# Filter transform of a long convolution: second stage issued for two groups at a time, with more places for its buffers

## The chip, the cores and the metric

One Trainium2 chip, one of its cores. The metric is the device time of one execution in microseconds. The kernel before takes 899.78 us (median of three runs, 898.28 to 901.48).

## What is computed

```python
def _attn_ref(x, v, pos_emb, w1, w2):            # x, v: 4 x 12608 x 128
    h_mlp = np.maximum(pos_emb @ w1, 0.0) @ w2   # a filter of 12608 points for each of 128 channels
    h_filt = h_mlp * np.exp(-0.01 * pos)[:, None]
    u = x * v
    Uf = np.fft.rfft(u, n=2 * S, axis=1)
    Hf = np.fft.rfft(h_filt, n=2 * S, axis=0)
    y = np.fft.irfft(Uf * Hf[None], n=2 * S, axis=1)[:, :S]
    return x * y
```

The result then goes through a small expert layer: per batch the 128 rows with the highest score are put through two matrices (1024 wide) and added back. All of it is fp32.

## The kernel before, in words

The long transforms are split into two short ones by a two-factor index map (101 by 125 points), done as matmuls. Channels go in 32 **groups** of four. The program has four parts, one after the other: (1) the filter's values (`h_hid`, to about 33 us); (2) the **filter transform** (`h_spec`, about 33 to 110 us), which the change touches; (3) the main loop over 4 batches x 32 groups, which transforms, multiplies with the stored filter spectrum and transforms back; (4) the choice of rows and the expert layer, spread over the main loop, the last of it behind it.

`h_spec` does this for each group g:

- **fold** (L373, GpSimd; the first four on VectorE): adds and subtracts mirrored halves of the filter into one of four places `fb`.
- **First stage F(g)** (`fwd`, L382): 16 fp32 matmuls of 101 columns, recorded as 32 rows of the trace, into two PSUM banks: the pair a0, a1 for even g, c1 for odd g. ScalarE copies both banks to SBUF, `te` (L385, two copies). Then fold(g + 4) is issued.
- **Second stage S(g)** (L402): 64x64 tiles on four quarters of the array, here 8 fp32 matmuls of 202 columns (16 rows of the trace), from `te` into `p` and `q`, the two banks of c2 for even g and of c0 for odd g.
- ScalarE copies q to `qs` (L404). VectorE then does four operations, two of them with a mirrored operand: L407, L408 (in place on p), and twice L410, which read p and write the sums `ht`. SyncE stores `ht` to DRAM (`hd`, L411), from where the main loop loads it again.

TensorE runs its instructions in program order, so S(g) stands behind F(g + 1), and S(g) may write p only after VectorE has finished with S(g - 2) in the same banks. PSUM is full: a0, a1 (one bank each), c0, c1, c2 (two each). SBUF has two places for `te` and two for `ht`.

The main loop's first steps use the same banks: the first transform f(0) (L426) writes a0, a1, is copied by ScalarE (L428), and the second transform D(0) (L268) writes c1. VectorE then works on it (L435 to L447); D(1) goes to c0, D(2) to c1 again, f(1) and f(2) between them. From D(2) on TensorE also runs the inverse transforms (L263).

Of the kernel before, what the change touches and what calls it, by code (L numbers as in the profile page):

```python
# [17 lines left out]
B, S, D, FO = 4, 12608, 128, 64  # L18
NQ = 64
N1, N2, N3 = 101, 250, 125  # L20
# [3 lines left out]
NG = 32  # L24
HC = 4 * N1
# [14 lines left out]
JH = (N3 + 1) // 2  # L40
# [13 lines left out]
OFF, _o = {}, 0  # L54
# [33 lines left out]
def _steps():  # L88
    j = np.arange(N3)
    first = -(-(N1 * N3 - N1 * j) // N3)  # L90
    blk = [slice(32 * k, min(32 * k + 32, N3)) for k in range(NB)]
    return first, [(c, int(first[c].min()), int(first[c].max())) for c in blk]
# [71 lines left out]
def hyena_moe(ctx, tc, xg, x2, pos, bw, ww, wg, mw1, mw2, fo, c1, gx, cf, ci, wm, tk, out):  # L164
    nc = tc.nc
# [6 lines left out]
    arena = cp.tile([128, ARENA], F32, name="arena")  # L172
    big = cp.tile([128, D * 2 * NJ], F32, name="big")

    def view(t, off, shape):
        n = int(np.prod(shape[1:]))
        r = t[:shape[0], off:off + n]
        if len(shape) > 2:
            ax = "abcd"[:len(shape) - 1]
            r = r.rearrange(f"p ({' '.join(ax)}) -> p {' '.join(ax)}", **dict(zip(ax[1:], shape[2:])))  # L180
        return r

    def buf(name, k, shape):
        o, n, w = OFF[name]
        return view(arena, o + k % n * w, shape)
# [7 lines left out]
    def ps1(k, shape, name):  # L193
        return view((*bank1, *bank2[::2])[k], 0, shape)

    def ps2(k, shape, name):
        return view(bank2[k], 0, shape)
# [29 lines left out]
    hb = view(big, 0, [N1, 2, D, N3 + 1])  # L227
    fo_sb = view(arena, OFF["wx"][0] + 32 * JH, [128, 2, NQ])
    fbo = [OFF["wx"][0], OFF["wx"][0] + 16 * JH] + [OFF["xa"][0] + k * 8 * D for k in (2, 3)]
    hd = dp.tile([128, NG, 2 * HC], F32, name="hd")  # L230
    blk = [c for c, _, _ in _steps()[1]]

    def rev(t):
        return t.rearrange("p (s i) -> p s i", i=N1)[:, :, ::-1]

    def nat(t):
        return t.rearrange("p (s i) -> p s i", i=N1)

    def load_u(t):
        b, g = divmod(t, NG)  # L240
        if b < B:
            for k, n in enumerate("xv"):
                nc.sync.dma_start(buf(n, t, [NP, XC]), xg[b, :, g, k])

    def stage_u(t):
        if t >= B * NG:
            return
        x, v = buf("x", t, [NP, XC]), buf("v", t, [NP, XC])
        nc.gpsimd.tensor_tensor(out=x, in0=x, in1=v, op=ALU.mult)  # L249

    def load_h(t):
        if t < B * NG:
            nc.sync.dma_start(buf("ht", t, [128, 2 * HC]), hd[:, t % NG])

    def mm2(o, lhsT, rhs, **kw):
        kw = kw or dict(start=True, stop=True)
        w = 32 if spare[0] else NQ
        for a in range(0, 128, w):
            nc.tensor.matmul(o[a:a + w], lhsT=lhsT[:, a:a + w], rhs=rhs, **kw)
# [94 lines left out]
    def h_spec():  # L354
        te = {}

        def tps(g):
            if g % 2:
                t = ps2(1, [128, 2, 512], f"htp_{g}")
                return [t[:, e, :HC] for e in range(2)]  # L360
            return [ps1(e, [128, HC], f"htp_{g}_{e}") for e in range(2)]

        def pqs(g):
            t = ps2(0 if g % 2 else 2, [128, 2, 512], f"hpq_{g}")
            return [t[:, e, :HC] for e in range(2)]

        def fold(g, eng=nc.gpsimd):
            if g >= NG:
                return
            fb[g] = view(arena, fbo[g % 4], [N1, 2, 2, 4, JH])  # L370
            hg = hb[:, :, 4 * g:4 * g + 4]
            for k, op in enumerate((ALU.add, ALU.subtract)):
                eng.tensor_tensor(out=fb[g][:, k], in0=hg[:, :, :, :JH], in1=hg[:, :, :, N3:JH - 1:-1], op=op)  # L373

        def fwd(g):
            b = fb.pop(g)
            tp = tps(g)
            t = te[g] = buf("te", g, [128, 2, HC])
            for e in range(2):
                for s in range(4):  # L380
                    for w in range(2):
                        nc.tensor.matmul(tp[e][w * NQ:w * NQ + JH, s * N1:(s + 1) * N1], lhsT=b[:, w ^ e, e, s], rhs=c1_sb[:N1, 0],  # L382
                                         start=True, stop=True)
            for e in range(2):
                nc.scalar.copy(out=t[:, e], in_=tp[e])  # L385
            fold(g + 4)

        fb = {}
        for g in range(4):
            fold(g, nc.vector)  # L390
        fwd(0)
        for g in range(NG):
            if g + 1 < NG:
                fwd(g + 1)
            p, q = pqs(g)
            t = te.pop(g)
            for h in range(2):
                c = slice(h * 2 * N1, (h + 1) * 2 * N1)
                for e in range(2):
                    for w, o in enumerate((p, q)):  # L400
                        r = slice(w * NQ, w * NQ + JH)
                        nc.tensor.matmul(o[e * NQ:(e + 1) * NQ, c], lhsT=fo_sb[r, e], rhs=t[r, e, c], start=True, stop=True)  # L402
            qs = buf("qs", g, [128, HC])
            nc.scalar.copy(out=qs, in_=q)  # L404
            vs = buf("yz", g, [128, HC])
            ht = buf("sd", g, [128, 2, HC])
            nc.vector.tensor_tensor(out=nat(vs), in0=rev(p), in1=nat(qs), op=ALU.subtract)  # L407
            nc.vector.tensor_tensor(out=nat(p), in0=nat(p), in1=rev(qs), op=ALU.add)  # L408
            for e, op in enumerate((ALU.add, ALU.subtract)):
                nc.vector.tensor_tensor(out=ht[:, e], in0=p, in1=vs, op=op)  # L410
            nc.sync.dma_start(hd[:, g], ht.rearrange("p e c -> p (e c)"))  # L411
            if NG - 5 <= g < NG - 3:
                stage_u(g - NG + 5)
                load_u(g - NG + 7)
            if g == NG - 2:
                stage_u(2)
            if g >= NG - 3:
                load_h(g - NG + 3)
# [487 lines left out]
    class Experts:  # L906
# [36 lines left out]
        def second(self, yp, hs, c0, c1):  # L943
            for c in range(c0, c1):
                mm2(yp, hs[:, c], self.m2[:, c], start=(c == 0), stop=(c == 7))
# [85 lines left out]
    for t in bank2[2:] + bank1 + bank2[:2]:  # L1031
        nc.vector.memset(t, 0.0)
    h_hid()
    h_spec()
    ex = None
    te, uv, ys, sd, ph = {}, {}, {}, {}, {}
# [3 lines left out]
    for t in range(NT + LAG):  # L1040
        g = t % NG
# [3 lines left out]
        if t < NT:  # L1045
            pq = ps2(1 - t % 2, [128, 2, 512], f"pq_{t}")
# [18 lines left out]
            o = t - 1 in uv  # L1065
# [37 lines left out]
        if i >= 0 and i % NG in LA:  # L1103
            if i % NG == LA[0]:
                ph[b] = P1(b)
            k, e = divmod(LA.index(i % NG), 2)
# [42 lines left out]
def build(inputs):  # L1149
    import concourse.bacc as _bacc  # L1150
    nc = _bacc.Bacc("TRN2", target_bir_lowering=False, num_devices=1, dynamic_dma_scratch_size=4096)
    arrays, args = {}, []
    for name, a in _layout(inputs):
        arrays[f"in_{name}_dram"] = a
        args.append(nc.dram_tensor(f"in_{name}_dram", a.shape, mybir.dt.from_np(a.dtype), kind="ExternalInput").ap())
    args.append(nc.dram_tensor("out_0_dram", (B, PR, NJ, D), F32, kind="ExternalOutput").ap())
    with tile.TileContext(nc) as tc:
        hyena_moe(tc, *args)
    return nc, arrays
# [7 lines left out]
```

## Time and profile before

| | |
|---|---|
| median of three runs | 899.78 us |
| the profiled execution, its own time | 897.32 us |
| its span (first to last instruction) | 895.5 us |
| TensorE busy | 865.7 us, 97% of the span |
| VectorE busy | 807.6 us, 90% |
| filter transform, first to last L402 | 36.38 to 110.85 us |
| DMA over the span | 214 GB/s |

A row of the timeline gives the start, the length, the engine, the line of the kernel, the operation with out<-in and the shapes, how many instructions were merged (x...), and in brackets how long the engine stood idle before and what ended that. PE is TensorE, DVE is VectorE, ACT is ScalarE, POOL is GpSimd. A matmul's modelled end lies after the start of the next, so lengths of merged rows overlap; paces are read from starts.

### The profile page before, as it was taken

The page shows a single profiled execution, that of the slowest core. Times are in us where ns is not written, and L with a number is a line of the kernel's source. Part 1 is how long each engine was busy: PE and PEld are TensorE (multiplying, and loading weights), DVE is VectorE, ACT ScalarE, POOL GpSimd, SP SyncE. Part 2 cuts the span into 40 slices and gives each one's busy share as a digit, 9 for nine tenths or more (in the row PEclk, how much of TensorE's full clock was granted, in tenths as well). Part 3 has the DMA queues.
Part 4 walks back from the last instruction along what each step waited for, and adds up shares of the span by engine and source line. Part 5 has one row for each costly group of instructions (what it writes and reads, how often), then busy time and mean ns, then how long its engine had stood idle before and what let it go on. Part 6 is the DMA issues. An engine that isn't in the chain of part 4 may idle for free.

```text
span 895.5 us, 46412 instructions
## 1 busy us (share of the span) xinstructions
PE 865.7 (97%) x19606; PEld 763.4 (85%) x19606; DVE 807.6 (90%) x1543; ACT 627.9 (70%) x2242; POOL 763.9 (85%) x834
## 2 busy tenths in 40 slices
PE   8999989999999999999999999999999999999965
PEld 6788768999999889888899798888998898879954
DVE  8998899999999899999998898999998989997883
ACT  6655575555558988885579798855698888646920
POOL 5898659999999889898999798999998989988710
PEclk9999999999999999999999999999999999999996
DMA  7044587777887967688779766788797767855810
GB/s 251 35 174 172 205 291 226 213 217 230 262 248 246 296 219 220 200 247 250 243 234 299 224 213 207 231 247 236 250 300 237 221 199 227 253 176 179 267 60 7
DMA packets 83512, 195.06 MB, mean 218 GB/s; under 512 B 9639, under 2 KB 46608, under 8 KB 83304
## 3 DMA queue, kind: packets, MB, share of 16 engines
q1 hardware_dynamic: 83048, 191.57, 67.6%
q8 instruction: 154, 2.52, 1.1%
q0 software_dynamic: 256, 0.52, 0.2%
q14 instruction: 54, 0.44, 0.2%
HBM read 151.46 MB, written 40.60 MB: 214 GB/s over the span
## 4 chain that ended last, share of the span: by engine, by line
PE 71%; DVE 16%; ACT 5%; POOL 4%; issue 3%; DMA 2%; POOLq 0%; DVEq 0%; SPq 0%; ACTq 0%
PE c L263 19%; PE a L426 15%; PE c L268 15%; ACT arena L601 4%; PE c L546 3%; PE a L542 3%; PE a L546 3%; PE c L542 3%; PE c L402 2%; PE a L382 2%; DVE arena L440 2%; DVE c L441 2%; PE c L382 2%; DVE arena L446 1%; DVE ms L696 1%
## 5 line engine op out<-in xcount | busy, mean ns | idle before, releaser
L263 PE MATMUL c<-ci_sb,arena 128*26 128x126 f32 x8128 | 261.0, 271 | 2.1 <-POOL arena L453 1.6
L263 PEld LDWEIGHTS c<-ci_sb,arena 128*26 128x26 f32 x8128 | 244.7, 104 | 5.1 <-POOL arena L453 1.8
L268 PE MATMUL c<-arena,cf_sb 128*32 128x404 f32 x2048 | 214.0, 502 | 3.3 <-ACT arena L428 1.3
L426 PE MATMUL a<-c_sb,arena 128*32 128x202 f32 (+1 forms) x4096 | 216.1, 334 | 0.0
L426 PEld LDWEIGHTS a<-c_sb,arena 128*32 128x32 f32 (+1 forms) x4096 | 174.5, 108 | 26.7 <-issue 12.8
L249 POOL TENSOR_TENSOR arena<-arena 128x500 f32<-128x500 f32 x128 | 161.9, 1265 | 11.3 <-DMA arena<-in_xg_dram 11.3
L428 ACT COPY arena<-a 128x404 f32<-128x404 f32 x256 | 128.1, 501 | 50.2 <-PE a L426 48.8
L477 ACT COPY big<-c 128x824 f32<-128x824 f32 x127 | 106.3, 837 | 78.2 <-PE c L263 77.9
L453 POOL TENSOR_TENSOR arena<-arena 128x404 f32<-128x404 f32 x127 | 124.0, 977 | 39.0 <-DVE arena L447 30.7
L601 ACT ACTIVATE arena<-arena 128x128 f32<-128x128 f32 x502 | 147.4, 299 | 11.7 <-DVE arena L591 9.5
L268 PEld LDWEIGHTS c<-arena,cf_sb 128*32 128x32 f32 x2048 | 100.8, 109 | 35.6 <-issue 18.8
L440 DVE TENSOR_TENSOR arena<-c,arena 128x808 f32<-128x808 f32 x127 | 126.8, 998 | 3.8
L441 DVE TENSOR_TENSOR c<-c,arena 128x808 f32<-128x808 f32 x127 | 126.7, 998 | 0.0
L454 POOL TENSOR_TENSOR arena<-arena 128x404 f32<-128x404 f32 x127 | 123.6, 973 | 0.0
L601 ACT ACTIVATION_READ_ACCUMULATOR arena<-arena 128x1 f32 x502 | 96.0, 191 | 0.0
L529 POOL TENSOR_TENSOR arena<-big 128x512 f32<-128x512 f32 x72 | 89.8, 1285 | 0.7 <-PE c L542 0.4
L446 DVE TENSOR_TENSOR arena<-c,arena 128x404 f32<-128x404 f32 x127 | 73.6, 579 | 12.9
L435 DVE TENSOR_TENSOR c<-c,arena 128x404 f32<-128x404 f32 x128 | 74.6, 583 | 11.6 <-ACT arena L271 8.2
L432 DVE TENSOR_TENSOR c<-c,arena 128x404 f32<-128x404 f32 x128 | 75.0, 586 | 9.6 <-ACT c L765 4.9
L497 POOL TENSOR_TENSOR big<-big,arena 128x184 f32<-128x184 f32 x128 | 74.5, 582 | 10.0
L271 ACT COPY arena<-c 128x404 f32<-128x404 f32 x128 | 63.6, 497 | 24.2 <-PE c L268 23.1
L496 POOL TENSOR_TENSOR big<-big,arena 128x184 f32<-128x184 f32 x128 | 75.0, 586 | 1.3 <-ACT arena L478 1.3
(196 smaller groups left out, 1433.5 us busy)
## 6 DMA issues: line engine op xcount, KB each, us to landing
arena<-in_xg_dram SPq DMA_DIRECT2D x256, 250.0 KB, 3.9
arena<-hd SPq DMA_DIRECT2D x128, 404.0 KB, 4.5
out_dram<-arena SPq DMA_DIRECT2D x60, 420.0 KB, 5.4
arena<-in_x_dram SPq DMA_DIRECT2D x36, 420.0 KB, 4.7
hd<-arena SPq DMA_DIRECT2D x32, 404.0 KB, 3.0
arena<-in_x_dram SPq DMA_DIRECT2D x48, 210.0 KB, 5.0
arena<-in_pos_dram SPq DMA_DIRECT2D x15, 202.0 KB, 4.5
arena<-in_x_dram SPq DMA_DIRECT2D x4, 315.0 KB, 4.5
```

The costliest lines, as they stand in the source:

```text
L249: nc.gpsimd.tensor_tensor(out=x, in0=x, in1=v, op=ALU.mult)
L263: nc.tensor.matmul(o[32 * k:32 * k + c.stop - c.start], lhsT=lhsT[:, c], rhs=rhs, start=True, stop=True)
L268: nc.tensor.matmul(pq[w][a:a + 32], lhsT=cf_sb[:, 2 * w + a // NQ, a % NQ:a % NQ + 32], rhs=te[:, a // NQ], start=True, stop=True)
L426: nc.tensor.matmul(tps[s // 2][c, s % 2], lhsT=u[:, s, c], rhs=c1_sb[:, 0:k + 2:k + 1], start=True, stop=True)
L428: nc.scalar.copy(out=te[:, :, 2 * h:2 * h + 2].rearrange("p e s i -> p s e i"), in_=tps[h])
L440: nc.vector.tensor_tensor(out=mt, in0=uv, in1=ht[:, 0].unsqueeze(1).to_broadcast([128, 2, HC]), op=ALU.mult)
L441: nc.vector.tensor_tensor(out=uv, in0=uv, in1=ht[:, 1].unsqueeze(1).to_broadcast([128, 2, HC]), op=ALU.mult)
L453: eng.tensor_tensor(out=nat(sd[:, 0]), in0=nat(yz[:, 0]), in1=rev(yz[:, 1]), op=ALU.add)
L454: eng.tensor_tensor(out=nat(sd[:, 1]), in0=rev(yz[:, 0]), in1=nat(yz[:, 1]), op=ALU.subtract)
L477: nc.scalar.copy(out=ay[:, t % NG, :NJ + JM, ss], in_=o3[:, :, :NJ + JM].rearrange("p s x -> p x s"))
L529: nc.gpsimd.tensor_tensor(out=cm[:, e].rearrange("p j (g s) -> p j g s", s=4), in0=av[0], in1=av[1], op=op)
L601: nc.scalar.activation(out=x, in_=x, func=AF.Copy, accum_out=self.sc[:, j:j + 1])
```

## The change

The first stage runs two groups ahead in pairs: after the start, TensorE's order is F(2j+2), F(2j+3), S(2j), S(2j+1) instead of F(g+1), S(g). The second stage does all 404 columns in one matmul (4 instead of 8 matmuls for a group). `te` gets four places and `ht` gets four; the two new places of `te` and one of `ht` lie in a part of the arena that the main loop uses later, one of `ht` in the main loop's `mt`. The PSUM banks of both stages, the folds, ScalarE's and VectorE's operations and the stores stay as they are.

```diff
     fbo = [OFF["wx"][0], OFF["wx"][0] + 16 * JH] + [OFF["xa"][0] + k * 8 * D for k in (2, 3)]
+    teo = [OFF["te"][0], OFF["te"][0] + 2 * HC] + [OFF["xa"][0] + k * 8 * D for k in (0, 1)]
+    hto = [OFF["sd"][0], OFF["mt"][0], OFF["xa"][0] + 4 * 8 * D, OFF["sd"][0] + 2 * HC]
...
         def fwd(g):
             b = fb.pop(g)
             tp = tps(g)
-            t = te[g] = buf("te", g, [128, 2, HC])
+            t = te[g] = view(arena, teo[g % 4], [128, 2, HC])
...
-        fwd(0)
+        def second(g):
+            t = te.pop(g)
+            pq[g] = pqs(g)
+            for e in range(2):
+                for w, o in enumerate(pq[g]):
+                    r = slice(w * NQ, w * NQ + JH)
+                    nc.tensor.matmul(o[e * NQ:(e + 1) * NQ], lhsT=fo_sb[r, e], rhs=t[r, e], start=True, stop=True)
+
+        pq = {}
+        ahead = {0: (0, 1), 1: (2,), 2: (3, 4), 3: (5,)}
         for g in range(NG):
-            if g + 1 < NG:
-                fwd(g + 1)
-            p, q = pqs(g)
-            t = te.pop(g)
-            for h in range(2):
-                c = slice(h * 2 * N1, (h + 1) * 2 * N1)
-                for e in range(2):
-                    for w, o in enumerate((p, q)):
-                        r = slice(w * NQ, w * NQ + JH)
-                        nc.tensor.matmul(o[e * NQ:(e + 1) * NQ, c], lhsT=fo_sb[r, e], rhs=t[r, e, c], start=True, stop=True)
+            for k in ahead.get(g, (g + 2, g + 3) if g % 2 == 0 else ()):
+                if k < NG:
+                    fwd(k)
+            if g < 4:
+                second(g)
+            elif g % 2 == 0:
+                second(g)
+                second(g + 1)
+            p, q = pq.pop(g)
             qs = buf("qs", g, [128, HC])
             nc.scalar.copy(out=qs, in_=q)
             vs = buf("yz", g, [128, HC])
-            ht = buf("sd", g, [128, 2, HC])
+            ht = view(arena, hto[g % 4], [128, 2, HC])
```

TensorE in the middle of the filter transform, before: F(6), S(5), F(7), and the first matmul of S(6). a0 and a1 are one bank each, c0 to c2 two banks each, and the brackets name the engines whose semaphores the row waits for.

```order
L382 MATMUL a0_70<-c1_sb_80,arena_68 63x101 [waits Pool_49] x2
L382 MATMUL a0_70<-c1_sb_80,arena_68 63x101 x6
L382 MATMUL a1_71<-c1_sb_80,arena_68 63x101 x8
L402 MATMUL c0_72<-arena_68 64x202 [waits DVE_49,Activation_49]
L402 MATMUL c0_72<-arena_68 64x202
L402 MATMUL c0_72<-arena_68 64x202 [waits Activation_49]
L402 MATMUL c0_72<-arena_68 64x202 x5
L382 MATMUL c1_73<-c1_sb_80,arena_68 63x101 [waits Pool_49] x2
L382 MATMUL c1_73<-c1_sb_80,arena_68 63x101 x14
L402 MATMUL c2_74<-arena_68 64x202 [waits DVE_49,Activation_49]
```

The same place after the change: F(8), F(9), S(6), S(7).

```order
L384 MATMUL a0_70<-c1_sb_80,arena_68 63x101 [waits Activation_49,Pool_49]
L384 MATMUL a0_70<-c1_sb_80,arena_68 63x101 [waits Pool_49]
L384 MATMUL a0_70<-c1_sb_80,arena_68 63x101 x6
L384 MATMUL a1_71<-c1_sb_80,arena_68 63x101 [waits Activation_49]
L384 MATMUL a1_71<-c1_sb_80,arena_68 63x101 x7
L384 MATMUL c1_73<-c1_sb_80,arena_68 63x101 [waits Activation_49,Pool_49]
L384 MATMUL c1_73<-c1_sb_80,arena_68 63x101 [waits Pool_49]
L384 MATMUL c1_73<-c1_sb_80,arena_68 63x101 x14
L399 MATMUL c2_74<-arena_68 64x404 [waits DVE_49,Activation_49]
L399 MATMUL c2_74<-arena_68 64x404 x3
L399 MATMUL c0_72<-arena_68 64x404 [waits DVE_49,Activation_49]
L399 MATMUL c0_72<-arena_68 64x404 x3
```

The two second stages now stand side by side, each with a wait of its own for VectorE, and the two first stages stand ahead of both.

TensorE at the end of the filter transform, before: the last first stage F(31), then S(30) and S(31), then the main loop's f(0) (L426).

```order
L382 MATMUL c1_73<-c1_sb_80,arena_68 63x101 [waits Pool_49] x2
L382 MATMUL c1_73<-c1_sb_80,arena_68 63x101 x14
L402 MATMUL c2_74<-arena_68 64x202 [waits DVE_49,Activation_49]
L402 MATMUL c2_74<-arena_68 64x202
L402 MATMUL c2_74<-arena_68 64x202 [waits Activation_49]
L402 MATMUL c2_74<-arena_68 64x202 x5
L402 MATMUL c0_72<-arena_68 64x202 [waits DVE_49,Activation_49]
L402 MATMUL c0_72<-arena_68 64x202
L402 MATMUL c0_72<-arena_68 64x202 [waits Activation_49]
L402 MATMUL c0_72<-arena_68 64x202 x5
L426 MATMUL a0_70<-c1_sb_80,arena_68 32x202 [waits Pool_49]
```

The same place after the change: the last matmuls of F(31), then S(28), S(29), S(30), S(31), then f(0) (L436 there).

```order
L384 MATMUL c1_73<-c1_sb_80,arena_68 63x101 x14
L399 MATMUL c2_74<-arena_68 64x404 [waits DVE_49,Activation_49]
L399 MATMUL c2_74<-arena_68 64x404 x3
L399 MATMUL c0_72<-arena_68 64x404 [waits DVE_49,Activation_49]
L399 MATMUL c0_72<-arena_68 64x404 x3
L399 MATMUL c2_74<-arena_68 64x404 [waits DVE_49,Activation_49]
L399 MATMUL c2_74<-arena_68 64x404 x3
L399 MATMUL c0_72<-arena_68 64x404 [waits DVE_49,Activation_49]
L399 MATMUL c0_72<-arena_68 64x404 x3
L436 MATMUL a0_70<-c1_sb_80,arena_68 32x202 [waits Pool_49]
```

Four second stages with no first stage between them now stand ahead of the main loop's first matmuls; before there were two.

## Rows read from the trace of the kernel before

**Rows 1.** The profile's page, part 1: busy time, share of the span and instructions of each engine.

```profile
PE 865.7 (97%) x19606; PEld 763.4 (85%) x19606; DVE 807.6 (90%) x1543; ACT 627.9 (70%) x2242; POOL 763.9 (85%) x834
```

**Rows 2.** Timeline of TensorE, 59.9 to 64 us, one round of the filter transform.

```profile
61.06 1.61 PE L382 MATMUL a<-c_sb,arena 101*63 101x101 f32 x32
62.59 0.92 PE L402 MATMUL c<-arena 63*64 63x202 f32 x16
63.44 0.74 PE L382 MATMUL c<-c_sb,arena 101*63 101x101 f32 x12
```

**Rows 3.** Timeline of TensorE, 61.44 to 62.22 us, a piece from the middle of one first stage (12 pairs of matmuls, two side by side).

```profile
61.19 1.21 PE L382 MATMUL a<-c_sb,arena 101*63 101x101 f32 x24
```

**Rows 4.** Timeline of TensorE, 33 to 50 us, the start of the filter transform: a single matmul of the first stage, the first S(0), and S(4).

```profile
34.73 0.25 PE L382 MATMUL c<-c_sb,arena 101*63 101x101 f32 x1
...
36.38 0.92 PE L402 MATMUL c<-arena 63*64 63x202 f32 x16
...
45.91 0.92 PE L402 MATMUL c<-arena 63*64 63x202 f32 x16
```

**Rows 5.** Timeline of VectorE, 57.4 to 64.8 us, three groups of the filter transform and the start of a fourth.

```profile
57.42 0.57 DVE L407 TENSOR_TENSOR arena<-c,arena 128x404 f32<-128x404 f32 x1
...
59.62 0.57 DVE L407 TENSOR_TENSOR arena<-c,arena 128x404 f32<-128x404 f32 x1
...
60.85 1.06 DVE L410 TENSOR_TENSOR arena<-c,arena 128x404 f32<-128x404 f32 x2
61.83 0.57 DVE L407 TENSOR_TENSOR arena<-c,arena 128x404 f32<-128x404 f32 x1
...
64.15 0.58 DVE L407 TENSOR_TENSOR arena<-c,arena 128x404 f32<-128x404 f32 x1
```

**Rows 6.** Timeline of ScalarE, 62.7 to 64.2 us, the copy of q.

```profile
63.62 0.50 ACT L404 COPY arena<-c 128x404 f32<-128x404 f32 x1 [0.36 <-PE c L402]
```

**Rows 7.** Timeline of GpSimd, 62.5 to 68 us, the two folds of one group.

```profile
62.82 2.09 POOL L373 TENSOR_TENSOR arena<-big 101x504 f32<-101x504 f32 x2 [0.29 <-PE a L382]
```

**Rows 8.** Timeline of VectorE, 34 to 54 us: the first operation of groups 0, 1 and 5.

```profile
38.63 0.56 DVE L407 TENSOR_TENSOR arena<-c,arena 128x404 f32<-128x404 f32 x1
...
40.83 0.57 DVE L407 TENSOR_TENSOR arena<-c,arena 128x404 f32<-128x404 f32 x1
...
49.85 0.58 DVE L407 TENSOR_TENSOR arena<-c,arena 128x404 f32<-128x404 f32 x1
```

**Rows 9.** Timeline of VectorE, 101 to 117 us, the end of the filter transform: first operation of group 29, sums of groups 29, 30 and 31 with two waits for stores, and the main loop's first operation.

```profile
107.50 0.57 DVE L407 TENSOR_TENSOR arena<-c,arena 128x404 f32<-128x404 f32 x1
...
108.72 1.06 DVE L410 TENSOR_TENSOR arena<-c,arena 128x404 f32<-128x404 f32 x2
...
112.61 1.06 DVE L410 TENSOR_TENSOR arena<-c,arena 128x404 f32<-128x404 f32 x2 [1.72 <-DMA hd<-arena]
...
115.31 1.06 DVE L410 TENSOR_TENSOR arena<-c,arena 128x404 f32<-128x404 f32 x2 [0.53 <-DMA hd<-arena]
116.29 0.58 DVE L435 TENSOR_TENSOR c<-c,arena 128x404 f32<-128x404 f32 x1
```

**Rows 10.** Timeline of TensorE, 105 to 128 us: S(30), S(31), f(0), D(0), f(1), D(1), D(2), then f(3), the first inverse transform and D(3).

```profile
107.98 0.92 PE L402 MATMUL c<-arena 63*64 63x202 f32 x16
109.93 0.92 PE L402 MATMUL c<-arena 63*64 63x202 f32 x16 [1.04 <-DVE arena L410]
110.78 1.58 PE L426 MATMUL a<-c_sb,arena 128*32 128x202 f32 x32
113.02 1.56 PE L268 MATMUL c<-arena,cf_sb 128*32 128x404 f32 x16 [0.66 <-ACT arena L428]
114.40 1.56 PE L426 MATMUL a<-c_sb,arena 128*32 128x202 f32 x32
116.62 1.56 PE L268 MATMUL c<-arena,cf_sb 128*32 128x404 f32 x16 [0.66 <-ACT arena L428]
...
120.67 1.56 PE L268 MATMUL c<-arena,cf_sb 128*32 128x404 f32 x16 [1.11 <-DVE arena L447]
122.03 1.59 PE L426 MATMUL a<-c_sb,arena 128*32 128x202 f32 x32
123.39 1.95 PE L263 MATMUL c<-ci_sb,arena 128*26 128x126 f32 x64
125.12 1.57 PE L268 MATMUL c<-arena,cf_sb 128*32 128x404 f32 x16
```

**Rows 11.** Timeline of TensorE, 799 to 811 us, the end of the main loop.

```profile
803.71 0.42 PE L263 MATMUL c<-ci_sb,arena 128*26 128x126 f32 x8 [1.56 <-POOL arena L453]
804.63 3.10 PE L263 MATMUL c<-ci_sb,arena 128*26 128x126 f32 x56 [0.50 <-POOL arena L454]
807.48 2.25 PE L263 MATMUL a<-ci_sb,arena 128*26 128x126 f32 x64
```

**Rows 12.** The same place in stretches; the columns are the stretch, its length, PE busy (x instructions), granted clock (PEclk, 1.00 is 2.4 GHz), DMA share, GB/s.

```profile
804.00:805.00 1.00, 0.50 (x18) 0.87 0.00 0
805.00:808.00 3.00, 3.00 (x64) 0.50 0.02 5
```

**Rows 13.** The stores of the sums (L411): time from issue to landing.

```profile
DMA to landing us min/median/max: 2.3/3.0/4.9
```

## The prediction

> **What bounds the kernel now.** First the page's busy times: TensorE 865.7 us, VectorE 807.6 us [rows 1]. An average over all stages says little of the filter transform, so I read the timelines there. TensorE runs without a gap in it: F at 61.06, S at 62.59, the next F at 63.44 [rows 2], so a group costs 1.53 + 0.85 = 2.38 us. VectorE, when it has work waiting, starts a group every 2.20 us (57.42, 59.62, 61.83) and then waits a little for the next (64.15, 2.32 later) [rows 5]. So TensorE sets the pace, with VectorE only 8% behind. GpSimd needs 2.09 us for a group's two folds, plus 0.29 us of waiting [rows 7]; it follows.
>
> At the end that order is turned round. VectorE waits 1.72 and 0.53 us for stores of earlier sums, which still hold the two places of `ht` [rows 9], and S(31) starts 1.04 us late, at 109.93, because VectorE's sums of group 29 end only at 108.72 + 1.06 = 109.78 [rows 9, 10]. From there TensorE's chain goes S(31) 109.93, D(0) 113.02, D(1) 116.62, D(2) 120.67, D(3) 125.12 [rows 10]. D(2) is where the main loop's steady round of 4.45 us begins (120.67 to 125.12), and TensorE sets that. So I price the change as a shift of D(2).
>
> **The change, part by part.**
>
> *One matmul of 404 columns.* A slot of the first stage (two matmuls side by side) takes (1.21 - 0.25)/11 = 0.087 us [rows 3, 4]; 16 slots are 1.39 of the 1.53. A slot of 202 columns takes 1.36/8 = 0.17, one of 404 takes 1.36/4 = 0.34 (122.03 to 123.39 and 120.67 to 122.03) [rows 10]. S now has four slots of 202, 0.68 of its 0.85; two slots of 404 are 0.68 again. What goes is a part of the remaining 0.17: the train D(0), begun from idle, takes 1.38 (113.02 to 114.40), 0.02 over its slots, so some of the entry is hidden by longer slots. I take 0.82 for S alone (bounds 0.70 and 0.85).
>
> *Pairs.* Two F in a row: 1.53 + 1.39 = 2.92, if the seam between them is as smooth as the slots inside one (no row shows this seam; with an entry for each it is 3.06). Two S in a row: 0.82 + 0.68 = 1.50. A pair is then 4.42 us of TensorE, 2.21 a group instead of 2.38. The Trainium skill's page "TensorEngine Tiling (Array Packing)", section "Tiling Modes", says that a change of tiling mode drains TensorE; the 0.14 us of F and 0.17 us of S that lie over the slots agree with it, and by that rule alone the change is a gain of 0.17 us a group.
>
> *The wait that takes its place.* PSUM is not enlarged. S(g) still waits for VectorE's last operation on g - 2 in the same two banks, as the rows of the order show for both matmul trains of a pair. S(2j+1) now stands right behind S(2j), but VectorE starts on 2j only when it is through with 2j-1, whose banks S(2j+1) wants. So S(2j+1) comes when VectorE ends 2j-1, and both first stages of the next pair, and S(2j+2) behind them, are queued behind it on TensorE. The circle, from VectorE's start of odd group o to its start of group o+4:
> - VectorE from its start to the end of its sums: 59.62 to 60.85 + 1.06 = 61.91, 2.29 [rows 5];
> - from there to S(o+2): 109.78 to 109.93, 0.15 [rows 9, 10];
> - S(o+2) alone 0.82, then two F 2.92, then S(o+3) starts;
> - from the start of S to VectorE's start on it, with the copy of q between: 62.59, 63.62, 64.15, so 1.56 [rows 2, 5, 6]; 1.55 with 404 columns;
> - VectorE on o+3: 2.20, then it starts o+4.
>
> Together 9.93 us for four groups, 2.48 a group. That is more than TensorE's 2.38 now, so the pairs make the stage slower; TensorE stands idle 9.93 - 2 x 4.42 = 1.09 us in every second pair.
>
> *The start.* S(0) stays at 36.38 and VectorE's first two groups at 38.63 and 40.83 [rows 4, 8]. The new order then gives F(2), S(1), F(3), F(4), S(2) at 36.38 + 0.82 + 1.53 + 0.82 + 2.92 = 42.47, F(5) and S(3) at 44.82, F(6), F(7), S(4) at 44.82 + 0.82 + 2.92 = 48.56, where it was 45.91 [rows 4]. VectorE starts group 4 at 48.56 + 1.55 = 50.11 and group 5 at 52.31; before that was 49.85 [rows 8]. It starved while two F ran ahead: 2.46 us late.
>
> *To the end.* From group 5 to 29 are six circles, 59.58 us: start 111.89, sums through at 114.18, S(31) at 114.33. Before, S(31) was at 109.93, so +4.40. F(30) and F(31) are over by then, so S(30) and S(31) each only wait for VectorE, and f(0) is queued behind them. D(0) to D(2) then follow at the distances they have now [rows 10], +3.09, +3.60, +3.60 (ScalarE's copies set them), D(2) at 124.62. Before it was held 0.45 us beyond that distance, at 120.67, by VectorE, which began the main loop at 116.29 behind its late stores [rows 9, 10].
>
> *Four places for the sums.* Those waits go: a store lands in 2.3 to 4.9 us [rows 13], and a place is now wanted again only after four groups, over 8.8 us. That returns the 0.45 us, counted already. New places shared with the main loop cost nothing: `mt` is written some 6 us after the store of group 29 is issued. A longer landing would cost its excess.
>
> *Moved with F:* two ScalarE copies of 0.50 us each and the fold. ScalarE then has four copies before the two of q, 3.0 of 4.42 us. The four fold operations of a pair take 4.18 of 4.42 us on GpSimd, and their results are wanted two pairs later. On SyncE's queue the loads of x and the filter sums stay behind the stores of groups 27 to 31, which all come later; f(2) still has them in time, as it is later too.
>
> **Sum.** D(2) moves from 120.67 to 124.62: +3.9 us, made of +2.46 (start), +1.94 (24 groups) and -0.45 (stores). The profiled execution of 897.32 us would be 901.2; on the median of 899.78, 2.46 above it, 903.7. Below or above 0.3% (2.7 us) is about what a measurement of this kernel can tell from no change.
>
> **Bounds.** If the switches cost nothing any more (F pair 2.78, S 0.70), the circle is 9.67 and the start 1.1 us shorter: D(2) about +1.2, 901.0. If the seam costs a full entry (3.06) and S stays at 0.85, the circle is 10.10 and the start 0.4 longer: +5.3, 905.1.
>
> **Rivals.**
>
> *TensorE's clock falls at the new gap (slower still).* In the last pair S(29) is through at about 109.6; S(30) comes at 112.1, S(31) at 114.3. That is some 2.5 and 1.4 us of idleness around 0.8 us of work. At the end of the main loop 1.56 and 0.50 us of idleness around eight matmuls were followed by a granted clock of 0.50 (1.2 GHz), and the 56 matmuls of L263 then took 2.85 us [rows 11, 12] where 64 take 1.73 [rows 10]: 1.34 us lost. Here S(31) and f(0), 0.82 + 1.36, would run at the lower level: 1.3 to 2.2 us more, 905.4. Against it: S(31)'s wait of 1.04 us did no harm before. The Trainium skill's page "TensorE: Matmul & The Clock Gate", Part 1, says that an idle array is gated to half its clock and that activity gives it back; the 0.50 there agrees with that, and it speaks against this change.
>
> *Faster: VectorE back to back.* If S(2j+1) did not hold up the queue, VectorE would run at 2.20 from group 5 on: sums of 29 through at 52.31 + 24 x 2.20 + 2.29 = 107.40, S(31) at 107.55, D(2) at 117.84, -2.8 us: 896.9. It decides where the circle is under 2 x 4.42 = 8.84, that is 1.09 us shorter than I make it; none of its five terms has that much to give.
>
> *No change that can be measured.* The low bound above, or half of the starvation at the start being made good: +1 to +2.5, about 901.5.
>
> **How the numbers follow.** The forecast as worked, 903.7 with its own range of 902.6 to 905.1: 0.45. With the clock's fall: 0.25. No measurable change: 0.22. Faster: 0.08. Slower by over 0.3% is thus 0.69 (some of the forecast's low side counts as no change), the same 0.23. The range reaches from the low bound less some scatter of the runs, 900.4, to the clock's price with some of the high bound, 906.2.
>
> **What would show it.** In the trace after: L417 starts every 2.20, 2.20, 2.20 and then about 3.3 us; every second odd S waits about 1.1 us for L420; no wait of L420 for a store; S(30) and S(31) wait 2.5 and 1.4 us; D(2) near 124.6 and rounds of 4.45 from there. The forecast is wrong if L417 comes every 2.2 us throughout, if S(4) starts before 47, or if the granted clock falls behind 109 us.

## The result, and the profile after

The changed kernel takes 905.17 us (median of four runs, 903.96 to 906.95), the kernel before beside it 899.03 (four runs, 897.26 to 901.48): a ratio of 1.0068 [1.0044, 1.0091], so some 0.7% slower. The ratios here and below are those on record; they differ a little from the quotients of the medians. The forecast was 903.7 with a range of 900.4 to 906.2.

The profiled execution of the changed kernel took 906.95 us, the slowest of its four, with a span of 905.2. Some 2.0 us of that lie ahead of the change's first row: S(0) starts at 38.37 and not at 36.38 [rows 4], in a part that the change leaves alone. Over the ten profiles of this document S(0) comes anywhere from 36.2 to 39.2; what sets it is open. All places below are therefore counted from S(0), written +x.

Page, part 1, and TensorE's timeline at the start of the filter transform (S(0), then S(4) with S(5)):

```profile
PE 866.4 (96%) x19350; PEld 757.4 (84%) x19350; DVE 807.8 (89%) x1543; ACT 628.2 (69%) x2242; POOL 762.9 (84%) x834
...
38.37 0.91 PE L399 MATMUL c<-arena 63*64 63x404 f32 x8
...
50.65 1.59 PE L399 MATMUL c<-arena 63*64 63x404 f32 x16
```

TensorE is busy for as long as before [rows 1]; what came in is idleness. VectorE's timeline, first operation of groups 2 and 4 to 8:

```profile
46.06 0.58 DVE L417 TENSOR_TENSOR arena<-c,arena 128x404 f32<-128x404 f32 x1 [0.95 <-ACT arena L414]
...
52.20 0.58 DVE L417 TENSOR_TENSOR arena<-c,arena 128x404 f32<-128x404 f32 x1 [1.47 <-ACT arena L414]
54.41 0.57 DVE L417 TENSOR_TENSOR arena<-c,arena 128x404 f32<-128x404 f32 x1
56.64 0.58 DVE L417 TENSOR_TENSOR arena<-c,arena 128x404 f32<-128x404 f32 x1
58.86 0.57 DVE L417 TENSOR_TENSOR arena<-c,arena 128x404 f32<-128x404 f32 x1
62.16 0.58 DVE L417 TENSOR_TENSOR arena<-c,arena 128x404 f32<-128x404 f32 x1 [1.02 <-ACT arena L414]
```

Twice it starves while two first stages run ahead (0.95 and 1.47 us), so group 5 starts at +16.04 where it was +13.47 [rows 4, 8]. Then come three steps of 2.2 us and one of 3.30, and that repeats to the end. TensorE at the same time: S(6), then S(7), which waits, then F and F, then S(8) and S(9) without a wait, and the next F:

```profile
55.09 0.91 PE L399 MATMUL c<-arena 63*64 63x404 f32 x8
56.85 0.91 PE L399 MATMUL c<-arena 63*64 63x404 f32 x8 [0.85 <-DVE arena L420]
57.69 1.61 PE L384 MATMUL a<-c_sb,arena 101*63 101x101 f32 x32
59.13 1.56 PE L384 MATMUL c<-c_sb,arena 101*63 101x101 f32 x32
60.62 1.59 PE L399 MATMUL c<-arena 63*64 63x404 f32 x16
62.13 1.61 PE L384 MATMUL a<-c_sb,arena 101*63 101x101 f32 x32
```

Of the two S at the top, the second stands 0.85 us for VectorE's sums (L420) of the group two back, and both F behind it wait too. A pair of F takes 2.93 (57.69 to 60.62), a pair of S 1.51. The end of the transform: S(28) with S(29), S(30), S(31), f(0), D(0), D(1), D(2):

```profile
110.41 1.59 PE L399 MATMUL c<-arena 63*64 63x404 f32 x16
114.40 0.91 PE L399 MATMUL c<-arena 63*64 63x404 f32 x8 [2.40 <-DVE arena L420]
116.60 1.38 PE L399 MATMUL c<-arena 63*64 63x404 f32 x8 [1.29 <-DVE arena L420]
117.91 2.73 PE L436 MATMUL a<-c_sb,arena 128*32 128x202 f32 x32
121.33 1.56 PE L270 MATMUL c<-arena,cf_sb 128*32 128x404 f32 x16 [0.68 <-ACT arena L438]
...
124.93 1.56 PE L270 MATMUL c<-arena,cf_sb 128*32 128x404 f32 x16 [0.66 <-ACT arena L438]
...
128.53 1.56 PE L270 MATMUL c<-arena,cf_sb 128*32 128x404 f32 x16 [0.66 <-ACT arena L438]
```

The same place in stretches (start and end, length, PE busy, granted clock, DMA share, GB/s):

```profile
112.00:115.00 3.00, 0.60 (x8) 1.00 0.85 280
115.00:117.00 2.00, 0.71 (x8) 0.98 0.95 295
117.00:120.00 3.00, 3.00 (x36) 0.50 1.01 361
120.00:123.00 3.00, 2.32 (x36) 0.95 0.99 380
```

S(31) comes at +78.23, before at +73.55 [rows 4, 10]: 4.68 later. From about 116.9, within S(31), to 120.3 the granted clock is 0.50 (1.2 GHz); f(0) takes 2.73 us where it took 1.58 [rows 10], and from S(31) to D(0) pass 4.73 us, before 3.09. D(2) is no longer held by VectorE: 0.66 us of waiting for ScalarE is the ordinary step. It comes at +90.16, before +84.29. So D(2) is 5.87 us late, and the medians differ by 6.1.

### The profile page after: what moved, and what is told of

The parts are those of the page before. It is cut to its first block, busy times and chain, and to the rows that moved or that the text cites. A ratio compares the mean times of both kernels' runs of the same rounds, so it can differ in the third digit from the quotient of the medians.

```text
span 905.2 us, 45883 instructions
## 1 busy us (share of the span) xinstructions
PE 866.4 (96%) x19350; PEld 757.4 (84%) x19350; DVE 807.8 (89%) x1543; ACT 628.2 (69%) x2242; POOL 762.9 (84%) x834
## 4 chain that ended last, share of the span: by engine, by line
PE 75%; DVE 14%; ACT 4%; issue 2%; POOL 2%; DMA 1%; POOLq 0%; DVEq 0%; SPq 0%; ACTq 0%
PE c L265 20%; PE a L436 17%; PE c L270 17%; PE c L556 4%; ACT arena L611 3%; PE a L552 3%; PE a L556 3%; PE c L552 3%; PE c L399 2%; PE a L384 2%; DVE arena L420 2%; PE c L384 2%; DVE c L451 1%; DVE arena L450 1%; DVE ms L706 1%
## 5 line engine op out<-in xcount | busy, mean ns | idle before, releaser
L265 PE MATMUL c<-ci_sb,arena 128*26 128x126 f32 (+1 forms) x8128 | 264.0, 270 | 3.7 <-issue 1.7
L436 PE MATMUL a<-c_sb,arena 128*32 128x202 f32 (+1 forms) x4096 | 219.6, 335 | 0.0
L270 PE MATMUL c<-arena,cf_sb 128*32 128x404 f32 x2048 | 216.4, 502 | 2.3 <-ACT arena L438 2.0
L436 PEld LDWEIGHTS a<-c_sb,arena 128*32 128x32 f32 (+1 forms) x4096 | 177.2, 109 | 26.7 <-issue 11.3
L270 PEld LDWEIGHTS c<-arena,cf_sb 128*32 128x32 f32 x2048 | 104.0, 109 | 32.3 <-issue 15.7
```

What stands on the lines that cost most here:

```text
L265: nc.tensor.matmul(o[32 * k:32 * k + c.stop - c.start], lhsT=lhsT[:, c], rhs=rhs, start=True, stop=True)
L270: nc.tensor.matmul(pq[w][a:a + 32], lhsT=cf_sb[:, 2 * w + a // NQ, a % NQ:a % NQ + 32], rhs=te[:, a // NQ], start=True, stop=True)
L436: nc.tensor.matmul(tps[s // 2][c, s % 2], lhsT=u[:, s, c], rhs=c1_sb[:, 0:k + 2:k + 1], start=True, stop=True)
```

## The experiments

Their expectations call the forecast's mechanism Theory 1: the second S of a pair stands on TensorE's queue until VectorE has freed its banks, VectorE starves at the start, and the clock's fall comes on top. The rival is that the pairs themselves cost something: the switches, the 404-column matmuls, or the places shared with the main loop.

All eight, with the ratio to the kernel before beside which each ran (27 and 35 runs of it, medians 900.75 and 900.16; for the row "after" the four runs above), and three places from its trace:

| kernel | S(31) | S(31) to D(0) | D(2) | against before | median, us | ratio |
|---|---|---|---|---|---|---|
| before | +73.55 | 3.09 | +84.29 | | | |
| after | +78.23 | 4.73 | +90.16 | +5.87 | 905.17 | 1.0068 [1.0044, 1.0091] |
| after, again | +78.23 | 4.72 | +90.15 | +5.86 | 905.40 | 1.0059 [1.0038, 1.0081] |
| third place | +71.50 | 4.56 | +83.26 | -1.03 | 898.85 | 0.9971 [0.9951, 0.9992] |
| fill | +78.25 | 3.08 | +88.54 | +4.25 | 905.52 | 1.0055 [1.0036, 1.0075] |
| fill, again | +78.22 | 3.09 | +88.51 | +4.22 | 904.19 | 1.0050 [1.0027, 1.0073] |
| wide, four places, old order | +72.91 | 3.08 | +83.21 | -1.08 | 899.01 | 0.9988 [0.9972, 1.0004] |
| third place, short lead | +68.57 | 3.07 | +79.06 | -5.23 | 895.31 | 0.9936 [0.9913, 0.9959] |
| short lead, two places | +76.60 | 3.09 | +86.89 | +2.60 | 901.59 | 1.0018 [0.9997, 1.0039] |
| two places for the sums | +78.22 | 4.73 | +90.16 | +5.87 | 904.87 | 1.0061 [1.0039, 1.0083] |

The shift of D(2) and the change of the time (the ratio less 1, of 900 us) go together to within some 1.6 us in every row, so D(2) is the place to read.

### A third place for the second stage

From group 8 on, c0, c1 and the pair a0, a1 take turns as the target of F and of the odd S; c2 stays with the even S. An odd S then no longer needs the banks that VectorE is still reading.

```diff
+        def turn(j):
+            return "cab"[j % 3]
...
         def tps(g):
-            if g % 2:
+            j = g // 2 - 1
+            if j < 4:
+                return place("ab"[g % 2], f"htp_{g}")
+            return place(turn(j + g % 2), f"htp_{g}")
...
-            t = ps2(0 if g % 2 else 2, [128, 2, 512], f"hpq_{g}")
+            if g % 2 == 0:
+                return place("d", f"hpq_{g}")
+            return place(turn(g // 2) if g // 2 >= 4 else "c", f"hpq_{g}")
```

> The changed kernel with one thing altered: from group 8 on, the second stage of the odd group of a pair no longer goes to c0 each time. It takes the two banks that the first stage ahead of it has just left (ScalarE has copied them), and the banks a0+a1, c1 and c0 go round among these. The order of the work, the 404 columns, the places in SBUF, all operations stay. Theory 1 (S of the odd group waits for VectorE to leave the same banks, and the next pair's first stages stand behind it): from group 8 on VectorE starts a group every 2.22 us without the 3.30 us step, no odd S waits for VectorE, S(31) comes about 71.5 us after S(0) where it is 78.2 now and 73.6 in the kernel before, D(2) about 82 us after S(0) where it is 90.2 now and 84.3 before; about 6 to 8 us faster than the changed kernel, 1 to 2.5 us faster than the kernel before (ratio 0.997 to 0.999). Theory 2 (the pairs themselves cost the time: wide matmuls, the places shared with the main loop, two copies and folds in a row): no more than 1 us below the changed kernel, ratio 1.005 to 1.008.

VectorE's timeline, first operations in the steady part, and TensorE towards the end (S(26) and S(27), then S(30) with S(31), f(0), D(0), D(2)):

```profile
66.28 0.58 DVE L427 TENSOR_TENSOR arena<-c,arena 128x404 f32<-128x404 f32 x1
68.50 0.57 DVE L427 TENSOR_TENSOR arena<-c,arena 128x404 f32<-128x404 f32 x1
70.72 0.58 DVE L427 TENSOR_TENSOR arena<-c,arena 128x404 f32<-128x404 f32 x1
```

```profile
100.27 0.91 PE L409 MATMUL c<-arena 63*64 63x404 f32 x8
101.00 0.86 PE L409 MATMUL a<-arena 63*64 63x404 f32 x8
...
108.70 2.50 PE L409 MATMUL c<-arena 63*64 63x404 f32 x16 [2.40 <-DVE arena L430]
111.13 2.30 PE L446 MATMUL a<-c_sb,arena 128*32 128x202 f32 x32
114.11 1.56 PE L270 MATMUL c<-arena,cf_sb 128*32 128x404 f32 x16 [0.68 <-ACT arena L448]
...
121.31 1.56 PE L270 MATMUL c<-arena,cf_sb 128*32 128x404 f32 x16 [0.66 <-ACT arena L448]
```

The step of 3.3 us is gone: VectorE starts a group every 2.22 us, no odd S waits for it (S(27), now in a0 and a1, follows S(26) at once), and S(31) comes at +71.50, as Theory 1 had it. With the same pairs, the same wide matmuls and the same shared places the kernel is now faster than before, so none of these explains the loss. S(30) still waits 2.40 us, and the clock still falls: the two S of the last pair take 2.43 us (108.70 to 111.13), and D(2) comes about 1.3 us later than expected.

### The gap filled

Matmuls that compute nothing, 101x101 in fp32, stand ahead of S(30) (8) and of S(31) (5). They end inside the two waits.

```diff
+        def fill(n):
+            w = c1_sb[:N1, 0]
+            o = ps1(0, [N1, N1], "fill")
+            for _ in range(n):
+                nc.tensor.matmul(o, lhsT=w, rhs=w, start=True, stop=True)
...
+                if g == NG - 2:
+                    fill(8)
                 second(g)
+                if g == NG - 2:
+                    fill(5)
                 second(g + 1)
```

> The changed kernel with fp32 matmuls that nobody reads (101x101, into a0) in TensorE's two gaps at the end of the filter transform: 8 ahead of S(30) and 5 ahead of S(31). Theory 1 (the granted clock falls there because TensorE stands idle for 2.40 and 1.29 us): granted clock 1.00 from 100 to 130 us, S(31) to D(0) 3.1 us where the changed kernel's trace has 4.73, and 1.6 us below the changed kernel, ratio to the kernel before about 1.005. If the fall came by chance of that one execution, or for another reason: S(31) to D(0) as in the changed kernel, or the time no lower than its 905.2, ratio 1.0068.

TensorE at the end (fill, S(30), fill, S(31), f(0), D(0), D(2)), and one stretch of it:

```profile
110.21 1.67 PE L405 MATMUL a<-c_sb 101*101 101x101 f32 x16
112.68 0.91 PE L399 MATMUL c<-arena 63*64 63x404 f32 x8 [0.81 <-DVE arena L430]
113.52 1.14 PE L405 MATMUL a<-c_sb 101*101 101x101 f32 x10
114.89 0.91 PE L399 MATMUL c<-arena 63*64 63x404 f32 x8 [0.23 <-DVE arena L430]
115.73 1.58 PE L446 MATMUL a<-c_sb,arena 128*32 128x202 f32 x32
117.97 1.56 PE L270 MATMUL c<-arena,cf_sb 128*32 128x404 f32 x16 [0.66 <-ACT arena L448]
...
125.18 1.56 PE L270 MATMUL c<-arena,cf_sb 128*32 128x404 f32 x16 [0.66 <-ACT arena L448]
```

```profile
115.00:118.00 3.00, 2.34 (x44) 1.00 1.02 354
```

S(31) comes no earlier (+78.25), but with idle stretches of 0.81 and 0.23 us the granted clock stays at 1.00, f(0) takes 1.58 us again, and D(2) is 1.62 us earlier than after the change. The times did not settle it: the ratio, 1.0055, is near the 1.005 expected, but the median, 905.52 us, is not below the changed kernel's 905.17, which the expectation had named as a sign of chance or another cause. So the changed kernel and this one ran again side by side.

> The changed kernel once more, unaltered, beside the runs below on one chip. Theory 1 (the granted clock falls in the gaps ahead of S(30) and S(31) in nearly every execution): S(31) to D(0) 4.6 to 4.8 us again, ratio 1.005 to 1.008, and 1 to 2 us above the run with filled gaps. If the fall was chance: S(31) to D(0) 3.1 us, and the same time as with filled gaps.

> The changed kernel with the two gaps filled once more, to be compared with the changed kernel on one chip. Theory 1: granted clock 1.00 from 100 to 130 us, D(2) 88.5 us after S(0), 1 to 2 us below the changed kernel's median. If the fall is rare without the profiler: the same median within 0.5 us.

The traces repeat: +90.15 with the clock down, +88.51 with it up. The medians, 905.40 and 904.19, lie 1.2 us apart in the right direction, but their intervals overlap. The clock's price is shown in the traces; the times only suggest it.

### Wide matmuls and four places, in the old order

The kernel before with the 404-column matmuls and with the four places each of `te` and `ht`; TensorE's order F(g + 1), S(g) stays.

```diff
-            t = te[g] = buf("te", g, [128, 2, HC])
+            t = te[g] = view(arena, teo[g % 4], [128, 2, HC])
...
-                        nc.tensor.matmul(o[e * NQ:(e + 1) * NQ, c], lhsT=fo_sb[r, e], rhs=t[r, e, c], start=True, stop=True)
+                    nc.tensor.matmul(o[e * NQ:(e + 1) * NQ], lhsT=fo_sb[r, e], rhs=t[r, e], start=True, stop=True)
...
-            ht = buf("sd", g, [128, 2, HC])
+            ht = view(arena, hto[g % 4], [128, 2, HC])
```

> The kernel before, in its own order F(g+1), S(g), with the other two parts of the change: 404 columns in the second stage, and four places each for te and for the sums at the same addresses as in the changed kernel. Theory 1: VectorE's waits for stores are gone, TensorE's round is 2.35 to 2.38 us, S(31) 72.3 to 73.0 us after S(0) (73.55 before), D(2) 82.5 to 83.3 (84.3 before): 1 to 1.8 us faster than the kernel before, ratio 0.998 to 0.999. Theory 2 (wide matmuls or shared places cost the time): slower than the kernel before, ratio 1.003 or more.

TensorE at S(31) and D(2):

```profile
109.63 0.91 PE L402 MATMUL c<-arena 63*64 63x404 f32 x8 [0.71 <-ACT arena L404]
...
119.92 1.56 PE L270 MATMUL c<-arena,cf_sb 128*32 128x404 f32 x16 [0.66 <-ACT arena L428]
```

The pace stays 2.38 us a group: S with wide matmuls takes 0.84 instead of 0.85. VectorE waits for no store any more, so S(31) comes 0.64 us earlier, and D(2) is not held: together 1.08 us. The row of S(31) names a copy of q, that of group 30 from other banks. What S(31) needs are VectorE's sums of group 29, read here in VectorE's timeline:

```profile
108.42 1.06 DVE L410 TENSOR_TENSOR arena<-c,arena 128x404 f32<-128x404 f32 x2
```

They end at 109.48, 0.15 us ahead of S(31), the same distance as before [rows 9, 10]. So S(31) most likely waits for the sums as before, only that these are no longer late. In the times the 1.08 us are 0.9988 [0.9972, 1.0004], not to be told from no change. The rest of the edit shows no cost, as priced.

### Third place and a shorter lead

The third place from the start on, and the first stage one pair less far ahead: F(g + 1), F(g + 2), S(g), S(g + 1) for even g.

```diff
-        ahead = {0: (0, 1), 1: (2,), 2: (3, 4), 3: (5,)}
+        ahead = {0: (0, 1), 1: (2,)}
         for g in range(NG):
-            for k in ahead.get(g, (g + 2, g + 3) if g % 2 == 0 else ()):
+            for k in ahead.get(g, (g + 1, g + 2) if g % 2 == 0 else ()):
                 if k < NG:
                     fwd(k)
-            if g < 4:
+            if g < 2:
                 second(g)
...
         def tps(g):
-            if g % 2:
+            if g < 3:
+                return place("ab"[g % 2], f"htp_{g}")
+            return place(turn(g // 2), f"htp_{g}")
...
-            t = ps2(0 if g % 2 else 2, [128, 2, 512], f"hpq_{g}")
+            return place("d" if g % 2 == 0 else "c" if g == 1 else turn(g // 2), f"hpq_{g}")
```

> The changed kernel with the third place for S as in the run above, from group 3 on, and with a shorter lead: the pairs begin at group 2, and the order is F(2j+1), F(2j+2), S(2j), S(2j+1), so that the first stage runs at most two groups ahead. Theory 1 (2.5 us of the loss come from VectorE starving at the start while first stages run ahead): VectorE starts group 5 about 14.4 us after S(0) (16.0 in the changed kernel, 13.5 before), then a group every 2.22 us, S(31) about 68.7 us after S(0), D(2) about 79 (84.3 before): about 5 us faster than the kernel before, ratio 0.994. Theory 2 (pairs cost the time): slower than the kernel before. If the start does not matter: as the run with the third place alone.

TensorE at the end (S(30) with S(31), f(0), D(2)):

```profile
107.08 1.59 PE L406 MATMUL c<-arena 63*64 63x404 f32 x16 [0.87 <-DVE arena L427]
108.60 1.58 PE L443 MATMUL a<-c_sb,arena 128*32 128x202 f32 x32
...
118.27 1.56 PE L270 MATMUL c<-arena,cf_sb 128*32 128x404 f32 x16 [0.88 <-DVE arena L464]
```

VectorE starves once instead of twice (group 5 at +14.34 instead of +16.04), runs at 2.22 us from group 2 on, and F(31) now stands in the last gap, so S(30) waits 0.87 us and the clock stays up. S(31) and D(2) come at +68.57 and +79.06, within 0.2 of what was expected. At 895.31 us, 0.9936 [0.9913, 0.9959], this version beats both kernels.

### Shorter lead alone

The changed kernel with the two edits to `ahead` and `if g < 2` of the last diff; the PSUM places are its own.

```diff
-        ahead = {0: (0, 1), 1: (2,), 2: (3, 4), 3: (5,)}
+        ahead = {0: (0, 1), 1: (2,)}
...
-            for k in ahead.get(g, (g + 2, g + 3) if g % 2 == 0 else ()):
+            for k in ahead.get(g, (g + 1, g + 2) if g % 2 == 0 else ()):
```

> The changed kernel with the shorter lead alone: F(2j+1), F(2j+2), S(2j), S(2j+1) from group 2 on; the odd groups' S stay in c0 and wait for VectorE there. Theory 1 (start and circle are two separate losses): group 5 starts 14.4 us after S(0) as in the run with short lead and third place, but the step of 3.25 to 3.30 us comes back in every fourth group; S(31) 76.6 us after S(0) (78.2 in the changed kernel), D(2) 87 us after it, ratio 1.003 to 1.004. If the third place is not what removed the step: steps of 2.22 throughout and a ratio below 1.

TensorE, two odd S that wait:

```profile
60.53 0.91 PE L399 MATMUL c<-arena 63*64 63x404 f32 x8 [0.77 <-DVE arena L420]
...
70.49 0.91 PE L399 MATMUL c<-arena 63*64 63x404 f32 x8 [0.77 <-DVE arena L420]
```

They stand 9.96 us apart, four groups: the circle is there with either lead. The start costs 1.6 us less (group 5 at +14.42), the clock does not fall, and S(31) comes at +76.60 as expected. This separates the parts: from group 5 to S(31) pass 62.18 us here and 60.08 before [rows 4, 8, 10], so the circle by itself costs about 2.1 us. The ratio, 1.0018 [0.9997, 1.0039], came out below the 1.003 to 1.004 expected and can't be told from no change; the trace, D(2) at +86.89, is as expected.

### Two places for the sums

The changed kernel with the two old places of `ht`.

```diff
-            ht = view(arena, hto[g % 4], [128, 2, HC])
+            ht = buf("sd", g, [128, 2, HC])
```

> The changed kernel with two places for the sums again, as in the kernel before (te keeps four). Theory 1 (in the new order VectorE starves anyway, so waits for stores fall into its idle time): L420 waits for stores again in places, but S(31) stays within 0.8 us of 78.2 us after S(0), and the ratio is within 0.002 of the changed kernel's. If the two new places of the sums carry weight: 2 us or more above the changed kernel.

The waits over the filter transform (us in total, times, longest):

```profile
DVE arena L420 <- DMA hd<-arena: 2.5, 2, 1.4
```

TensorE at S(30) and S(31):

```profile
112.25 0.91 PE L399 MATMUL c<-arena 63*64 63x404 f32 x8 [1.35 <-DVE arena L420]
114.46 1.53 PE L399 MATMUL c<-arena 63*64 63x404 f32 x8 [1.29 <-DVE arena L420]
```

VectorE waits for stores again, twice, but S(31) and D(2) are where they were, +78.22 and +90.16: S(30)'s wait is shorter, S(31)'s the same, and the clock falls as before. D(2) waits the ordinary 0.66 us for ScalarE with two places as with four, so in the new order the four places carry nothing; the 0.45 us that the forecast credited to them comes with the order.

## Why the prediction was right, and where it was off

The direction and the mechanism were right, the size was not. The forecast as worked had a range of its own, 902.6 to 905.1, and 905.17 lies just outside it; the stated range holds it because it was stretched to the price of the rival that the clock falls, 905.4. That rival came true: the granted clock falls behind 109 us, which the prediction named as a sign that its forecast is wrong. The closeness of 905.17 to 903.7 is also in part luck, as the forecast was added to 899.78 and the kernel before ran at 899.03 this time: 3.9 us was forecast and 6.1 measured.

- **The place of the price** was right: the second S of a pair, standing on TensorE's queue for VectorE, with both F behind it. The third place takes that wait away and turns 1.0068 into 0.9971; that pairs, wide matmuls or shared places explain the loss falls with the same run.
- **The circle**: 9.93 us worked, 9.96 measured (52.20 to 62.16), with steps of 2.2, 2.2, 2.2 and 3.30. From group 5 to S(31) 62.19 us, worked 62.02. The wait of the odd S was forecast at about 1.1 us and its row shows 0.85, as that counts S(6) with its modelled length of 0.91; over the circle TensorE is idle for 9.96 - 2 x 4.44 = 1.08 us, worked 1.09.
- **The seam between two F** was taken as smooth, 2.92 for the pair; measured 2.93. S alone 0.82 against 0.84, S in pairs 1.50 against 1.51. The Trainium skill's page "TensorEngine Tiling (Array Packing)", section "Tiling Modes", says that a change of tiling mode drains TensorE, which makes fewer changes a gain; 2.22 us a group in the run with the third place, against 2.38 before, agrees.
- **The start**: 2.46 worked, 2.57 measured. S(4) was worked out 12.18 behind S(0) and came 12.28 behind it.
- **S(31)**: 4.40 worked, 4.68 measured, 2.57 + 2.11.
- **The stores**: -0.45 at D(2), as measured; but it is the order, not the places, that brings it, as the run with two places shows.
- **The clock** is the term that was mis-sized. The waits of S(30) and S(31) were forecast at 2.5 and 1.4 us and measured at 2.40 and 1.29, and the fall behind them was priced as 1.3 to 2.2 us and measured at 1.64. But it was a rival with a chance of 0.25 while the forecast kept the full clock, so D(2) was put 3.9 us late and was 5.87. What spoke for the full clock, that S(31)'s wait of 1.04 us did no harm before [rows 10], was a wait of less than half the length; the pair of waits 1.56 and 0.50, after which it did fall [rows 11, 12], was the nearer row.

3.95 as worked + 0.11 (start) + 0.17 (circle) + 1.64 (clock) is 5.87: nothing of the measured shift is left over.

The profiled execution's own time lies 9.6 us above that of before: 5.87 here, 2.0 ahead of S(0), and 1.8 somewhere behind D(2). Executions of one kernel differ there: the second profile of the changed kernel took 909.92 us, 3.0 more, with S(0) at 38.30 and D(2) at +90.15. The medians do not show the 1.8.

## What to carry to other kernels

When matmul trains of two kinds are put in pairs to save switches, count the buffers that the pair needs at once: with the old number of PSUM places the second train of a pair waits for the engine that drains the first one's predecessor, and all that is queued behind it waits too. Write the circle through that engine out from the durations in the trace before trusting the saving; here one more place for the drained banks turned the loss into a gain. And look at both ends of such a pipeline: the lead costs starvation at the start and leaves an unfilled gap at the end, where the clock can fall.

## What the runs showed of the hardware

- The granted clock fell to 0.50 while S(30) or S(31) ran in four profiles; TensorE had stood idle ahead of these two for 2.40 and 1.29 us (changed kernel, twice), for 2.40 (third place) and for 1.35 and 1.29 (two places for the sums). It stayed at 1.00 in the other six: idle for 1.04 us (before), 0.81 and 0.23 (fill, twice), 0.71 (wide), 0.87 and 1.23 (short leads). A fall cost 1.5 to 1.65 us up to D(0) each time. The Trainium skill's page "TensorE: Matmul & The Clock Gate", Part 1, has the clock fall for want of activity; these ten agree.
- The other fall in the main loop, the one at its end [rows 12], stands in the profile of before alone; in the other nine the granted clock is 1.00 there. The cause is open.
- TensorE's changes between F and S cost little: two groups take 2 x 2.38 = 4.76 us one by one [rows 2] and 2.93 + 1.51 = 4.44 in pairs, 0.16 a group for half of the changes.
